# One engine instead of two for the low parts of the expert weights: all subtracted on VectorE, none on GpSimd

## Chip, cores, metric

One core of one Trainium2 chip. The metric is the device time of one execution in microseconds (us), median over repeated executions.

## What is computed

Three layers in a row. A clustered attention over `q`, `k`, `v` (2 x 8 heads, 768 positions, 64 wide) gives 1536 tokens of 512. A dense layer, 512 to 2048 and back, follows. The third layer routes each token to one of eight experts or past all of them; this is where the change lies:

```python
do_compute = x @ w_skip > 0
xc = x[do_compute]
logits = xc @ w_gate
e_idx = argmax(logits, axis=1); gate_w = softmax(logits)[e_idx]
for e in range(8):
    mask = e_idx == e
    h = maximum(xc[mask] @ w1[e], 0)          # w1[e]: 512 x 1024
    y[mask] = gate_w[mask, None] * (h @ w2[e])  # w2[e]: 1024 x 512
out = x.copy(); out[do_compute] = xc + y
```

## The kernel before

Everything is written out by hand in program order; each engine runs its own instructions strictly in that order, and semaphores hold one engine for another.

**Precision.** Matrix products in the two expert layers run in a rounded 32-bit type (`fp32r`). To keep accuracy each operand is held as two numbers: a high part, the rounded copy, and a low part, the source minus the high part. A product is then three matmuls: high x high, high x low, low x high. For weights, ScalarE (ACT) makes the high part by a copy (line 919), and VectorE (DVE) or GpSimd (POOL) the low part by a subtraction (line 921). In names of the profile `xh`, `phi` are high parts, `xl`, `plo` low parts, both in the third layer eight buffers in turn (six are reused from the first layer's tokens, two are new, `phi`/`plo`); `rawa`, `rawb` are the weights as loaded.

**The third layer.** An expert's weights are four chunks of 128 x 4 x 512 numbers, 1 MB each: two of `w1`, two of `w2`. The work is a list of 32 *stages*, one chunk each: `u` (up: tokens times half of `w1`, lines 1069 to 1081) and `d` (down: activations times half of `w2`, line 1105). The order is up of expert 0, then up of expert 1, down of expert 0, up of 2, down of 1, and so on, with the eighth expert at the end; a leftover tile of 32 tokens (`xx_...`) is computed on an expert chosen at run time ahead of the last one. In the loop over stages (line 1268 on) one turn does, in this order: the 12 matmuls of the stage on TensorE (PE); on `u` stages the transposes of the previous expert's activations (`h_trans`: PE, high part on ACT, low part `hTl` on DVE); on `d` stages the combine `y` (DVE, line 1112) with its scatter (POOL, line 1114) or the transposed tokens of an expert two later (`x_prep`, low part `xTl` on DVE); four steps of the remaining routing work (`extras`, small DVE operations such as `en` and `ohx`); and last the split of the chunk three stages ahead (`split_stage(n + 3)`).

**The split.** `split2` (line 913) cuts a chunk into two halves of 128 x 1024. A counter `n` runs over all halves. For each, ACT makes the high part and the low part goes to POOL where `n % 8` is in `pool_n`, else to DVE. Stages 0 and 1 are split during the end of the dense layer with `pool_n=range(8)`, all on POOL (lines 993, 1009); stage 2 with `pool_n=()` (line 1049); stages 3 to 31 are split in the loop with the default. After the split the chunk's buffer is refilled by a DMA on SP's queue (`refill`, line 546), for the chunk eight later; that DMA waits for the halves' subtractions. POOL's queue also holds the gathers of tokens (line 1039) and the scatters. Matmuls of a stage wait for its low parts, and the low parts of activations stand behind the splits on DVE.

The lines that set where a low part is made:

```python
            eng = nc.gpsimd if n % 8 in pool_n else nc.vector
            eng.tensor_tensor(out=lo, in0=src, in1=_f(hi), op=ALU.subtract)
```

Of the kernel before, what the change touches and what calls it, by code (L numbers as in the profile page):

```python
# [20 lines left out]
def _f(ap):  # L21
    return ap.bitcast(F32)
# [3 lines left out]
def kernel(  # L26
# [32 lines left out]
    def pool(name, side=None, **kw):  # L59
        return tc.alloc_tile_pool(name=name, side=side, bufs=1, reuse_waits="tile", **kw)  # L60
# [17 lines left out]
    def ps_m(shape, name, dt=F32):  # L78
        return psum.tile(shape, dt, tag="M", name=name, bufs=1)

# [1 line left out]
    ident = const.tile([P, P], F32, name="ident")  # L82
    make_identity(nc, ident)
    identb = const.tile([P, P], BF16, name="identb")
    nc.vector.tensor_copy(identb, ident)

# [1 line left out]
    HS = S // 2  # L88
    nat = {}
    first = {}  # L90
# [517 lines left out]
    pieces = [(c, a_) for c in range(2, 8) for a_ in range(4)]  # L608
# [16 lines left out]
    for s in range(NSTEP + 16):  # L625
        p, r = divmod(s, 12)
# [40 lines left out]
    for i in range(2):  # L667
        m1_up(i, ps_s("ups")[:, i, :])

# [1 line left out]
    att.release()  # L671
    psum.release()
    psum = pool("psum2", None, space=PSUM)
# [55 lines left out]

    NI = NBLK * NFC  # L730

# [1 line left out]
    EMPTY = 2048.0  # L733
    XP = 32
    wg = rt.tile([P, KD, 32], F32, name="wg")
# [166 lines left out]
        V.tensor_tensor(out=g, in0=g, in1=ga[:, 3, :], op=ALU.add)  # L902
        V.tensor_scalar(out=g, in0=g, scalar1=1.0 / 1024.0, scalar2=None, op0=ALU.mult)

# [1 line left out]
    xhb = xh.rearrange("p c n -> p (c n)").rearrange("p (k a f) -> p k a f", a=2, f=512)  # L906
    xlb = xl.rearrange("p c n -> p (c n)").rearrange("p (k a f) -> p k a f", a=2, f=512)
    NXB = KD * NTOK // 1024
# [1 line left out]
    pc_t = {}  # L910
    nsp = [0]

    def split2(e, r, pool_n=(1, 4, 6)):
        for j in range(2):
            n = nsp[0]
            nsp[0] += 1
            src = chunks[8 + 4 * e + r][:, 2 * j:2 * j + 2, :]
            hi, lo = his[n % len(his)], los[n % len(los)]
            nc.scalar.activation(out=hi, in_=src, func=AF.Copy)  # L919
            eng = nc.gpsimd if n % 8 in pool_n else nc.vector  # L920
            eng.tensor_tensor(out=lo, in0=src, in1=_f(hi), op=ALU.subtract)  # L921
            pc_t[e, r, 2 * j] = hi[:, 0, :], lo[:, 0, :]
            pc_t[e, r, 2 * j + 1] = hi[:, 1, :], lo[:, 1, :]
# [15 lines left out]
    def split_stage(n, hold=False, **kw):  # L939
        if n >= len(stages):  # L940
            return
        k_, e, h = stages[n]
        r = h if k_ == "u" else 2 + h
        split2(e, r, **kw)
        if not hold:
            refill(8 + 4 * e + r)
# [103 lines left out]
    m1.release()  # L1050
    wip[0].release()

# [1 line left out]
    m2 = pool("m2", "right")  # L1054
    for k_ in range(2):
        his.append(m2.tile([P, 2, 512], F32R, name=f"phi{k_}"))
# [217 lines left out]
    for n, (k_, i, h) in enumerate(stages):  # L1274
# [9 lines left out]
        else:  # L1284
            down_half(i, h)
            if h == 1:
                e = pos_of[i]
# [28 lines left out]
    with tc.For_i(0, nreg, 1):  # L1316
        nc.vector.tensor_scalar(out=itc, in0=itc, scalar1=1.0, scalar2=None, op0=ALU.add)
        for _ in pick_expert():
            pass
        e = NPOS  # L1320
        for r in range(4):
            load_chunk(8 + 4 * e + r)
        for _ in tile_list(iota1, 1):
            pass
        gather(e, xi[:, 0:1])
        x_prep(e)
        for r in range(2):
            split2(e, r)
            up_half(e, r)
        for r in range(2):  # L1330
            h_trans(e, r)
        for r in range(2):
            split2(e, 2 + r)
            down_half(e, r)
        combine(e, xgx, xi[:, 1:2])
# [27 lines left out]
```

## Time and profile before

| | |
|---|---|
| device time, median of 3 runs (us) | 721.02 (718.91 to 723.09) |
| span of the profiled execution (us) | 722.5 |
| PE busy | 662.2 us, 92% |
| DVE busy | 478.7 us, 66% |
| ACT busy | 420.0 us, 58% |
| POOL busy | 374.4 us, 52% |
| bytes read from HBM | 66.18 MB, 103 GB/s over the span |

The profile records one execution; of its time the page gives the span, from the first to the last instruction, which lies within the range of the three runs. Busy shares are means over the whole program, and its three layers use the engines differently: the attention ends near 330 us, the dense layer near 570, the third layer takes the rest. A stretch has to be read by itself. The page's chain that ended last holds only the final scatter and says nothing of the layer ahead of it. DVE is VectorE, ACT is ScalarE, POOL is GpSimd, PE is TensorE, SP is the queue that issues most DMAs.

### The profile page before, as it was taken

What the parts mean: (1) busy time and instruction counts of PE and PEld (TensorE: products, weight loads), DVE (VectorE), ACT (ScalarE), POOL (GpSimd) and SP (SyncE); (2) the same over time, 40 slices, a digit from 0 to 9 for tenths busy, and PEclk for the clock granted to TensorE, in tenths of its full rate; (3) what the DMA queues carried; (4) which work ended last, traced back from release to release, by engine and by line L of the source; (5) the groups of instructions that cost most, each with busy time, mean ns of one, the idle gap of its engine ahead of it and who ended that gap; (6) DMA issues with size and microseconds to landing.
All of it is one profiled execution on the core that took longest, in us unless ns stands there. A gap on an engine that the chain in (4) does not pass through costs nothing. (4 is left out here: it accounts for less than half of the span.)

```text
span 722.5 us, 10397 instructions
## 1 busy us (share of the span) xinstructions
PE 662.2 (92%) x3571; PEld 494.3 (68%) x3571; DVE 478.7 (66%) x861; ACT 420.0 (58%) x808; POOL 374.4 (52%) x327
## 2 busy tenths in 40 slices
PE   5899999999999996688899999999999898888895
PEld 4666666666666664566688887888887676666665
DVE  5967877687777788999823225432245459999963
ACT  5787887888887854344444444444443547446741
POOL 4454654646553346656674444454342586346843
PEclk9999999999999999899999999999999979889999
DMA  8643635437231024443002000042333388767950
GB/s 197 144 115 74 186 104 133 128 75 185 75 105 63 30 82 152 147 134 128 0 2 117 1 1 1 0 140 94 116 117 101 133 303 291 242 218 252 325 183 24
DMA packets 58773, 88.83 MB, mean 123 GB/s; under 512 B 26745, under 2 KB 30203, under 8 KB 58720
## 3 DMA queue, kind: packets, MB, share of 16 engines
q1 hardware_dynamic: 56688, 81.79, 36.8%
q0 software_dynamic: 2032, 6.37, 2.4%
q8 instruction: 29, 0.48, 0.3%
q14 instruction: 24, 0.20, 0.1%
HBM read 66.18 MB, written 8.45 MB: 103 GB/s over the span
## 5 line engine op out<-in xcount | busy, mean ns | idle before, releaser
L343 DVE TENSOR_REDUCE st<-sps 128x1 f32<-128x768 f32 x96 | 91.6, 955 | 54.2 <-PE sps L340 43.7
L389 ACT ACTIVATE pt<-tps 128x384 f32<-128x384 f32 x192 | 83.8, 491 | 32.5 <-PE tps L382 32.0
L692 DVE TENSOR_TENSOR g<-ups,lk 128x512 f32<-128x512 f32 x48 | 33.0, 688 | 97.4 <-ACT lk L691 97.3
L603 PE MATMUL ups<-xh,wloi 128*128 128x512 f32 x192 | 78.5, 409 | 15.6 <-POOL wloi L579 15.5
L354 ACT ACTIVATE pr<-sps,st 128x768 f32<-128x768 f32 x96 | 87.0, 906 | 8.5 <-DVE st L358 4.3
L579 POOL TENSOR_TENSOR wloi<-rawb,whii 128x512 fp32r<-128x512 f32 x36 | 50.3, 1399 | 76.2 <-ACT whii L577 76.2
L397 PE MATMUL avps<-pt,vnat 128*64 128x384 f32 x384 | 81.8, 510 | 0.0
L603 PE MATMUL ups<-xh,whii 128*128 128x512 f32 x192 | 77.5, 404 | 2.3 <-ACT whii L577 2.3
L367 POOL TENSOR_SCALAR pr<-pr,st 128x768 f32<-128x768 f32 x48 | 47.9, 999 | 60.1 <-DVE st L362 53.5
L382 PE MATMUL tps<-ident,pr 128*128 128x128 f32 x576 | 78.7, 273 | 0.0
L693 ACT ACTIVATE gh<-g 128x512 fp32r<-128x512 f32 x48 | 30.4, 633 | 80.7 <-DVE g L692 80.7
L603 PE MATMUL ups<-xl,whii 128*128 128x512 f32 x192 | 77.0, 401 | 0.0
L708 PE MATMUL acc<-whio,gh 128*128 128x512 f32 x184 | 73.9, 402 | 2.1 <-ACT gh L693 2.1
L708 PE MATMUL acc<-whio,gl 128*128 128x512 f32 x184 | 72.1, 392 | 0.6 <-POOL gl L695 0.6
L382 PEld LDWEIGHTS tps<-ident,pr 128*128 128x128 f32 x576 | 68.4, 140 | 5.6 <-ACT pt L389 1.2
L708 PE MATMUL acc<-wloo,gh 128*128 128x512 f32 x184 | 72.0, 391 | 0.0
L603 PEld LDWEIGHTS ups<-xh,wloi 128*128 128x128 f32 x192 | 37.6, 196 | 27.5 <-POOL wloi L579 19.8
L691 ACT ACTIVATE lk<-ups 128x512 f32<-128x512 f32 x48 | 28.4, 591 | 45.4 <-PE ups L603 45.4
L921 DVE TENSOR_TENSOR xl<-rawb,xh 128x1024 fp32r<-128x1024 f32 x26 | 52.7, 2052 | 1.3 <-ACT xh L919 1.3
L589 POOL TENSOR_TENSOR wloo<-rawb,whio 128x512 fp32r<-128x512 f32 x36 | 50.1, 1392 | 0.9 <-ACT whio L588 0.8
L603 PEld LDWEIGHTS ups<-xh,whii 128*128 128x128 f32 x192 | 37.3, 194 | 12.2 <-ACT whii L577 4.8
L603 PEld LDWEIGHTS ups<-xl,whii 128*128 128x128 f32 x192 | 37.2, 194 | 7.9
(293 smaller groups left out, 1487.9 us busy)
## 6 DMA issues: line engine op xcount, KB each, us to landing
rawb<-in_moe_w_dram SPq DMA_DIRECT2D x26, 1024.0 KB, 5.4
stg<-in_moe_w_in_dram SPq DMA_DIRECT2D x16, 512.0 KB, 4.2
stg<-in_moe_w_out_dram SPq DMA_DIRECT2D x16, 512.0 KB, 4.0
rawa<-in_moe_w_dram SPq DMA_DIRECT2D x8, 1024.0 KB, 7.4
vnat<-in_v_dram SPq DMA_DIRECT2D x8, 384.0 KB, 3.4
x_scratch<-x SPq DMA_DIRECT2D x6, 512.0 KB, 2.6
out_dram<-x SPq DMA_DIRECT2D x6, 512.0 KB, 3.6
UB<-UA SPq DMA_DIRECT2D x15, 192.0 KB, 3.0
```

Source lines behind the costliest of these rows:

```text
L343: nc.vector.tensor_reduce(out=st[:, 0:1], in_=ps[:, :, 0:HS], axis=AX.XY, op=ALU.max, negate=True)
L354: nc.scalar.activation(out=pr, in_=ps[:, :, 0:HS], func=AF.Exp, bias=st[:, 0:1], accum_out=st[:, 1:2])
L367: nc.gpsimd.tensor_scalar(out=pr, in0=pr, scalar1=st[:, 2:3], scalar2=0.0, op0=ALU.mult, op1=ALU.add)
L382: nc.tensor.transpose(ps[:, t, :], pr[:, kh, t * P:(t + 1) * P], ident)
L389: nc.scalar.activation(out=pt[:, 3 * kh:3 * kh + 3, j, :], in_=t_t[s][kh], func=AF.Copy)
L397: nc.tensor.matmul(av_t[g][64 * h:64 * h + 64, :], lhsT=vnat[p][:, h, kt, :], rhs=pt_t[p, half, h][:, kt].rearrange("p j c -> p (j c)"), s ...
L579: eng.tensor_tensor(out=lo, in0=src, in1=_f(hi), op=ALU.subtract)
L589: nc.gpsimd.tensor_tensor(out=lo, in0=src, in1=_f(hi), op=ALU.subtract)
L603: nc.tensor.matmul(ps, lhsT=w[:, cc, :], rhs=x[:, cc, cs], start=(n == 0), stop=(n == 3 * KD - 1))
L692: nc.vector.tensor_tensor(out=g, in0=ps, in1=t, op=ALU.max)
L708: nc.tensor.matmul(ps, lhsT=a[:, ts_], rhs=w, start=(fc == 0 and n == 0), stop=(fc == NFC - 1 and n == 2))
L921: eng.tensor_tensor(out=lo, in0=src, in1=_f(hi), op=ALU.subtract)
```

## The change

The default of one argument changes: in the loop over stages, and in the loop behind it that runs only when more tiles are left over, no half goes to POOL any more. The remaining edits remove comments.

```diff
-    def split2(e, r, pool_n=(1, 4, 6)):
+    def split2(e, r, pool_n=()):
         for j in range(2):
             n = nsp[0]
             nsp[0] += 1
```

What follows shows the order of instructions on two engines, each row a line of the kernel, an operation, what it writes and reads, and a count.

DVE at the turns of the first stages, where expert 1's up halves are multiplied; rows with + are of the change, with - of before (`plo_5985`, `plo_5987` are the two new low buffers):

```order
 L1067 TENSOR_TENSOR xTl<-xT,xTh 128x512
+L921 TENSOR_TENSOR plo_5985<-rawb,phi_5984 128x1024
 L921 TENSOR_TENSOR plo_5987<-rawb,phi_5986 128x1024
 L1081 TENSOR_SCALAR h<-hps 128x512
-L921 TENSOR_TENSOR xl<-rawb,xh 128x1024
+L921 TENSOR_TENSOR xl<-rawb,xh 128x1024 x2
 L1090 TENSOR_TENSOR hTl<-hT,hTh 128x512
```

Each chunk's two subtractions now stand together on DVE, ahead of the next `h` or `hTl`.

POOL from the end of the gathers to the second scatter, before:

```order
L1039 DMA xg<-x_scratch,idx_g 128x512 x6
L921 TENSOR_TENSOR plo_5985<-rawb,phi_5984 128x1024
L921 TENSOR_TENSOR xl<-rawb,xh 128x1024
L921 TENSOR_TENSOR xl<-rawa,xh 128x1024
L921 TENSOR_TENSOR plo_5985<-rawa,phi_5984 128x1024
L1114 DMA out_dram<-y,idx_s 1536x512
L921 TENSOR_TENSOR xl<-rawb,xh 128x1024 x2
L921 TENSOR_TENSOR plo_5985<-rawb,phi_5984 128x1024
L1114 DMA out_dram<-y,idx_s 1536x512
```

and POOL from the last work of the dense layer to the end, with the change:

```order
L921 TENSOR_TENSOR xl<-rawa,xh 128x1024 x4
L1039 DMA xg<-x_scratch,idx_g 128x512 x2
L546 DMA rawa<-in_moe_w_dram 128x4x512 x2
L1039 DMA xg<-x_scratch,idx_g 128x512 x6
L1114 DMA out_dram<-y,idx_s 1536x512 x4
L1230 DMA xxg<-x_scratch,xi 128x128
L1114 DMA out_dram<-y,idx_s 1536x512 x2
```

The 22 subtractions of the stage loop are gone from POOL; its four of stages 0 and 1 and its DMAs stay in their order. PE, ACT and SP keep theirs.

## Rows read from the trace of the kernel before

Times are microseconds from the start of the span unless marked ns.

**Rows 1.** Busy time by stretch: PE, PEld, DVE, ACT, POOL, clock, DMA share, GB/s; x is instructions.

```profile
core 0: us, PE busy (x) PEld busy (x) DVE busy (x) ACT busy (x) POOL busy (x), PEclk, DMA share, GB/s
580.00:600.00 20.00, 18.15 (x86) 14.70 (x85) 12.96 (x27) 10.31 (x15) 13.34 (x12) 0.85 0.93 335
600.00:620.00 20.00, 14.78 (x63) 11.45 (x62) 19.66 (x31) 10.66 (x13) 11.88 (x5) 0.83 0.69 240
620.00:640.00 20.00, 14.96 (x63) 11.77 (x62) 19.86 (x35) 9.85 (x12) 8.20 (x4) 0.84 0.64 227
```

**Rows 2.** Waits of PE from 589 to 716 us: total, times, longest.

```profile
PE yps L1105 <- DVE xl L921: 11.2, 3, 5.2
PE yps L1105 <- DVE hTl L1090: 5.5, 2, 3.3
```

**Rows 3.** Line 921 by engine: shortest/median/longest ns, first and last start.

```profile
L921 DVE TENSOR_TENSOR xl<-rawb,xh x26: 1206/1221/6486, 577.0 to 703.1; 128x1024 fp32r<-128x1024 f32 x26
...
L921 POOL TENSOR_TENSOR xl<-rawb,xh x10: 2364/2434/3449, 592.9 to 702.2; 128x1024 fp32r<-128x1024 f32 x10
```

**Rows 4.** Timeline 609.6 to 616.1 us: start, us, engine, line, idle before.

```profile
609.59 6.49 DVE L921 TENSOR_TENSOR xl<-rawb,xh 128x1024 fp32r<-128x1024 f32 x1
...
610.30 4.68 POOL L921 TENSOR_TENSOR xl<-rawb,xh 128x1024 fp32r<-128x1024 f32 x2
...
616.13 0.79 PE L1105 MATMUL yps<-xl,hTh 128*128 128x512 f32 x1 [5.22 <-DVE xl L921]
```

**Rows 5.** Stretches A and B: line 921 alone (DVE, POOL), then all engines.

```profile
589.11:647.09 57.98, 28.88 (x16) 25.89 (x10) 0.88 0.73 255
647.09:692.54 45.45, 35.08 (x16) 25.62 (x9) 0.96 0.78 274
...
589.11:647.09 57.98, 47.34 (x216) 37.41 (x215) 54.77 (x78) 33.33 (x40) 28.56 (x13) 0.88 0.73 255
647.09:692.54 45.45, 38.56 (x186) 29.22 (x188) 44.35 (x40) 29.85 (x37) 31.04 (x13) 0.96 0.78 274
```

**Rows 6.** Timeline of DVE from 636.2 to 640 us, no POOL subtract running.

```profile
636.23 0.86 DVE L1148 TENSOR_SCALAR ohx<-iotax,jt 128x128 f16<-128x128 f32 x4
637.01 2.34 DVE L921 TENSOR_TENSOR xl<-rawb,xh 128x1024 fp32r<-128x1024 f32 x2
639.28 0.68 DVE L1081 TENSOR_SCALAR h<-hps 128x512 f32<-128x512 f32 x1
639.88 0.67 DVE L1090 TENSOR_TENSOR hTl<-hT,hTh 128x512 fp32r<-128x512 f32 x1
```

**Rows 7.** Timeline of DVE: third and sixth combine.

```profile
646.43 0.74 DVE L1112 SCALAR_TENSOR_TENSOR y<-yps,gts,xg 128x512 f32<-128x512 f32 x1
...
691.87 0.75 DVE L1112 SCALAR_TENSOR_TENSOR y<-yps,gts,xg 128x512 f32<-128x512 f32 x1 [0.31 <-PE yps L1105]
```

**Rows 8.** Groups of DVE from 589 to 647 us: busy, mean ns, idle before.

```profile
L1148 DVE TENSOR_SCALAR ohx<-iotax,jt 128x128 f16<-128x128 f32 x12 | 7.5, 689 | 0.0
...
L1183 DVE TENSOR_TENSOR en<-en 128x1 f32<-128x1 f32 x7 | 3.6, 509 | 0.2
...
L1214 DVE TENSOR_SCALAR jt<-jt 128x12 f32<-128x12 f32 x1 | 2.1, 2095 | 0.0
```

**Rows 9.** Timeline of PE: first matmul of four stages.

```profile
598.03 0.48 PE L1105 MATMUL yps<-xh,hTh 128*128 128x512 f32 x1
...
604.13 0.39 PE L1076 MATMUL hps<-xh,xTh 128*128 128x512 f32 x1
...
660.70 0.39 PE L1076 MATMUL hps<-xh,xTh 128*128 128x512 f32 x1
...
667.01 0.48 PE L1105 MATMUL yps<-xh,hTh 128*128 128x512 f32 x1
```

**Rows 10.** Timeline: ScalarE's wait for a load; SP's last loads.

```profile
681.65 2.01 ACT L919 ACTIVATE xh<-rawa 128x1024 fp32r<-128x1024 f32 x2 [0.39 <-DMA rawa<-in_moe_w_dram]
...
693.76 0.93 SPq L546 DMA_DIRECT2D rawb<-in_moe_w_dram  x2
```

## Prediction

> **What bounds the kernel now.** The change touches only the second expert layer, so I went first to the table of busy time by stretch, for the last 140 us [rows 1]. Between 600 and 640 us VectorE (DVE) is busy 19.66 and 19.86 of 20 us, while TensorE (PE) has 14.78 and 14.96 and the granted clock falls to 0.83 and 0.84, a mix of its two levels (1.2 and 2.4 GHz). An engine as full as that sets the pace. The list of waits says what PE lacks there: 11.2 us in three waits for the low half `xl` of line 921, and 5.5 us in two for `hTl`, a low half of the activations, also made on DVE [rows 2].
>
> Next I asked whether DVE really does 20 us of work. The durations of line 921 say no: on DVE the shortest and the median of the largest group are 1206 and 1221 ns, but the longest is 6486 ns, for the same shape [rows 3]. The timeline around that longest one shows why. DVE starts it at 609.59; GpSimd (POOL) starts two subtracts of line 921 at 610.30 that last 4.68 us, to 614.98; DVE's one ends at 616.08, which is 1.10 us after that, about one undisturbed duration; and PE, idle 5.22 us, goes on at 616.13 [rows 4]. Nothing in the code makes the one subtract need the other. So in these rows a POOL subtract and a DVE subtract do not run beside each other: one holds the other up. POOL needs 2434 ns (median) for what DVE does in 1221 [rows 3].
>
> **What is removed.** 22 POOL subtracts vanish: 10 between 589.11 and 647.09 us (stretch A), the other 12 after it, 9 of them before 692.54 (stretch B); 25.89 + 25.62 us of POOL time go there [rows 5]. POOL keeps the four of stages 0 and 1, which run at the end of the first layer, and its indirect DMAs, which then stand behind fewer instructions and cost nothing new.
>
> **What is added.** 22 subtracts on DVE. Two back to back take 2.34 us, so one follows the next after about 1.14 us and is itself 1.21 long [rows 3, 6]. No semaphore is new to PE, but the order changes: `h`, `hTl`, `xTl` and `y`, in line on DVE, now always stand behind two subtracts, and on SP's queue the refill of a buffer waits for both of them. What that costs is DVE's time, counted next.
>
> Stretch A runs from the low half of expert 1's tokens to the end of the third combine (`y`, starts 646.43 [rows 7]). DVE is busy 54.77 of 57.98 us [rows 5]; it is the bound, so its time is the sum:
> - Line 921: 16 now take 28.88 us [rows 5]; 26 at 1.21 make 31.5: +2.6.
> - `ohx`: 12 take 7.5 us now [rows 8]; four undisturbed ones took 0.86 [rows 6], so 12 take 2.6: -4.9.
> - `en`, seven additions of one column, take 3.6 us at 509 ns each [rows 8]; another small one, `jt` at line 1214, takes 2.1 for 12 columns [rows 8]. Both stand where POOL subtracts run. At an estimated 0.15 each, from how little work there is against `ohx` at 0.215: -2.6 and -1.9.
> - Ten more instructions overlap their neighbours by 0.07: -0.7.
> - DVE's own idle time, 57.98 - 54.77 = 3.2 us, mostly waits for ScalarE that follow a stall of PE: about 0.7 stays, -2.5.
>
> That is -10.0. I take -9.5, since a few tenths must come back where DVE meets ScalarE's high half. The bounds of this term: -10.0 above, and -4.5 if each of the 26 came out at 1.4, a third of the way from the undisturbed 1.21 to the present mean of 28.88 / 16 = 1.8 (26 x 0.19 = 5 us lost). I take the undisturbed price because POOL has no other work here that lasts.
>
> Stretch B, three more experts up to the combine that starts at 691.87 [rows 7], is 45.45 us now. Three candidates for its new length:
> - DVE: per expert 8 subtracts x 1.14, four operations out of PSUM x 0.60 (`h` to `hTl` [rows 6]), one combine of 0.66 (it starts at 646.43 [rows 7], and A ends with it): 12.2; three times that and an estimated 0.8 for eight small operations at the end of the routing work: 37.3.
> - PE at its full clock: two up stages with their transposes from 660.70 to 667.01, two down stages with theirs from 598.03 to 604.13 [rows 9]: 6.31 + 6.10 = 12.4 per expert, 37.2 for three.
> - The weight loads: 274 GB/s x 45.45 us = 12.45 MB [rows 5]; at the 335 GB/s of 580 to 600 us [rows 1] that is 37.2. (The Trainium skill, DMA: Bandwidth & Descriptors, section Specifications, puts a core's limit at about 358 GB/s from HBM; by that figure the estimate would be 34.8 and the loads could not bind. No row holds that rate over such a stretch.)
>
> All three come out alike, so the gain is at most -8.0. I take -7.5: three chains so even will hold each other up a little. Its bounds are -8.0 and the -2.5 of rival 1. For A the same load sum is 255 x 57.98 = 14.8 MB, 44 us at 335 GB/s, below the 48 that DVE wants.
>
> After B come the last 30 us: the leftover tile of the expert, the last expert, the scatter and the end. There PE never waits on line 921 and DVE has gaps; three subtracts more, 3.6 us, lie in those gaps: 0. The last two weight loads leave at 693.76, right after PE's leftover-tile matmuls [rows 10], and move with PE.
>
> **Sum:** -9.5 - 7.5 + 0 = -17.0 us. The profiled execution spans 722.5 us, 1.5 above the median of the runs, 721.0; its rows carry over. 721.0 - 17.0 = **704.0**.
>
> **What is late next.** After the change no engine of this stretch is clearly slowest: DVE 12.2 per expert, PE 12.4, loads 12.4. ScalarE, some 30 us busy of 45 [rows 5], is no candidate.
>
> **Rivals.**
> 1. *The loads become the bound.* For: the load rate must rise from 274 to 334 GB/s (12.45 MB in 37.3 us) in B. The only long stretch that shows 335 had 93% of the transfer engines' time in use [rows 1], and no row shows that rate held for 100 us. Against: in the whole stretch ScalarE waits for a load once, 0.39 us [rows 10], and loads are asked for eight chunks, two experts, ahead. At 305 GB/s B takes 40.8 and A 48.5, giving 707; at 290, 42.9 and 51.0, giving -2.5 - 7.0, so 711.5. Middle **709**.
> 2. *Slower: DVE is simply full, and 22 more subtracts on it lengthen the layer.* If the long durations came from something that stays (the loads into SBUF, ScalarE's reads), the added ones would cost what the present ones do: 10 x 28.88/16 = 18.1 us in A and about 9 x 35.08/16 = 19.7 in B [rows 5], less 4.3 us of idle time: +33.5, so **754.5**. It decides from the point where 50 subtracts exceed the present 64.0 us and that idle time: a mean of (64.0 + 4.3) / 50 = 1.37 us. Against: undisturbed ones are 1.21, and the longest ends when POOL lets go [rows 3, 4, 6]. The Trainium skill takes both sides. Its page Perfetto Trace Analysis, section Optimizing Scalar/DVE Operations, says that with VectorE saturated, offloading work even to GpSimd may make sense, and that the port the two share may undo it; its first half speaks against this change and gives this rival. Its page SBUF — State Buffer, section Who interferes with whom, says that a VectorE instruction with two SBUF inputs and a GpSimd one that reads SBUF contend, and the loser blocks fully; by that the long durations go with POOL's subtracts and the forecast's -17 stands. This trace agrees with the second [rows 4].
> 3. *No change:* PE's waits for `xl` turn into waits for `hTl`, which now always stands behind two subtracts of DVE's own. It is in DVE's sum already, so it would need PE and DVE to wait for each other in turn: **720**.
>
> **Chances.** Forecast 0.72 (698 to 708), rival 1 0.18 (706 to 712), a part of the blocking staying 0.03 (712 to 717), rival 3 0.03, rival 2 0.04. A change of 0.5%, 3.6 us, is about what a measurement of this kernel can tell from none. Faster by more: 0.72 + 0.18 + 0.03 = 0.93; within it 0.03; slower 0.04.
>
> **Range.** Best case: PE never stalls. From 604.13 to 660.70 [rows 9] it does the twelve stages of three experts, which at its full clock are 37.2 us instead of 56.6: -19.4. The eight stages from there to 691.87 would be 24.8 instead of 31.2: -6.4. That floor, 695, leaves DVE's sum out, which ends at -18; the stretch ahead of 604 us and a shorter end could add a few us to it, so I go to 698. Worst of the likely cases: rival 1 at 290 GB/s, 711.5. So **698 to 712**.
>
> **What would show it.** In the profile after: every line 921 on DVE at 1.2 us, no duration over 1.5 after 590 us, and no POOL subtract there; `ohx` and `en` at 0.2 and 0.15; PE's waits for `xl` near 0; the granted clock near 1.0 from 600 to 640; three combines in some 38 us where [rows 7] have 45.4; the rate of the loads above 300 GB/s. The forecast is wrong if DVE's subtracts stay bimodal without POOL, if ScalarE's waits for loads grow to several us, or if PE's waits come back under another name.

## Result and the profile after

| | before | after |
|---|---|---|
| device time, median of 4 runs each (us) | 722.06 (718.91 to 723.38) | 702.82 (702.16 to 703.44) |
| span of the profiled execution (us) | 722.5 | 700.9 |
| DVE busy (us) | 478.7 | 465.7 |
| POOL busy (us) | 374.4 | 322.9 |

The ratio of after to before is 0.9746, 95% interval 0.9709 to 0.9782: 19.2 us less. DVE has 22 instructions more and is busy 13 us less.

Line 921 in the profile after, one row for each pair of buffers: shortest, median and longest duration in ns, then the first and last start.

```profile
L921 DVE TENSOR_TENSOR xl<-rawb,xh x36: 1212/1217/1227, 576.0 to 682.3; 128x1024 fp32r<-128x1024 f32 x36
...
L921 DVE TENSOR_TENSOR plo<-rawb,phi x8: 1215/1218/1227, 589.0 to 686.4; 128x1024 fp32r<-128x1024 f32 x8
L921 DVE TENSOR_TENSOR xl<-rawa,xh x8: 1210/1216/1225, 599.5 to 668.4; 128x1024 fp32r<-128x1024 f32 x8
L921 DVE TENSOR_TENSOR plo<-rawa,phi x8: 1209/1216/1226, 603.0 to 671.3; 128x1024 fp32r<-128x1024 f32 x8
L921 POOL TENSOR_TENSOR xl<-rawa,xh x4: 2372/2412/2419, 562.3 to 569.4; 128x1024 fp32r<-128x1024 f32 x4
```

Against [rows 3]: the spread is gone. All 60 subtracts on DVE last 1209 to 1227 ns; the long ones, up to 6486, went with POOL's. POOL keeps its four ahead of the layer.

The table by stretch (the columns of [rows 1]), and under it the two stretches of the prediction, A and B, at their new places: from the `xTl` at 588.04 to the end of the third combine at 635.83, and to that of the sixth at 673.06.

```profile
600.00:620.00 20.00, 19.26 (x91) 15.09 (x90) 19.62 (x43) 15.09 (x20) 1.03 (x1) 1.00 0.90 299
620.00:640.00 20.00, 17.93 (x88) 14.02 (x87) 19.93 (x40) 11.86 (x15) 1.99 (x2) 0.91 0.88 308
640.00:660.00 20.00, 20.00 (x97) 16.43 (x97) 20.00 (x22) 16.76 (x20) 5.42 (x2) 1.00 0.99 338
...
588.04:635.83 47.79, 44.98 (x214) 35.50 (x213) 46.98 (x88) 33.34 (x40) 2.75 (x3) 0.96 0.90 305
635.83:673.06 37.23, 37.23 (x206) 29.89 (x205) 37.16 (x49) 30.12 (x38) 9.27 (x4) 1.00 0.97 339
```

DVE is as full as before, but of work: A takes 47.79 us instead of 57.98 and B 37.23 instead of 45.45 [rows 5]. In B, PE is busy 37.23 of 37.23 us and DVE 37.16. Loads ran at 339 GB/s there with 97% of the transfer engines' time in use, and the granted clock is 1.00.

The waits of PE in the layer (total us, times, longest), against 11.2 and 5.5 us in [rows 2]:

```profile
PE yps L1105 <- DVE hTl L1090: 1.2, 1, 1.2
PE yps L1105 <- DVE xl L921: 0.8, 1, 0.8
PE yps L1105 <- DVE nxi L1200: 0.5, 1, 0.5
PE yps L1105 <- DVE exi L1134: 0.2, 1, 0.2
```

And on DVE's timeline the small operations that [rows 8] had at 7.5 and 3.6 us in all: eight `ohx`, and four of the seven `en`.

```profile
602.36 0.73 DVE L1183 TENSOR_TENSOR en<-en 128x1 f32<-128x1 f32 x4
...
621.25 1.68 DVE L1148 TENSOR_SCALAR ohx<-iotax,jt 128x128 f16<-128x128 f32 x8
```

### The profile page after: what moved, and what is told of

Read it like the earlier page. It is cut to its first block, busy times and chain, and to the rows that moved or that the text cites. A ratio compares the mean times of both kernels' runs of the same rounds, so it can differ in the third digit from the quotient of the medians.

```text
span 700.9 us, 10375 instructions
## 1 busy us (share of the span) xinstructions
PE 655.1 (93%) x3571; PEld 491.6 (70%) x3571; DVE 465.7 (66%) x883; ACT 419.9 (60%) x808; POOL 322.9 (46%) x305
## 5 line engine op out<-in xcount | busy, mean ns | idle before, releaser
L603 PE MATMUL ups<-xh,wloi 128*128 128x512 f32 x192 | 77.7, 405 | 15.9 <-POOL wloi L579 15.9
L691 ACT ACTIVATE lk<-ups 128x512 f32<-128x512 f32 x48 | 28.4, 592 | 49.0 <-PE ups L603 49.0
L603 PEld LDWEIGHTS ups<-xh,wloi 128*128 128x128 f32 x192 | 37.2, 194 | 26.5 <-POOL wloi L579 18.9
L1114 POOL DMA_INDIRECT out_dram<-y,idx_s x8 | 13.5, 1693 | 79.1 <-DVE y L1112 36.0
L603 PEld LDWEIGHTS ups<-xh,whii 128*128 128x128 f32 x192 | 37.2, 194 | 11.5 <-ACT whii L577 4.1
L921 DVE TENSOR_TENSOR xl<-rawb,xh 128x1024 fp32r<-128x1024 f32 x36 | 42.3, 1218 | 0.3 <-ACT xh L919 0.3
```

The source lines that it names most:

```text
L603: nc.tensor.matmul(ps, lhsT=w[:, cc, :], rhs=x[:, cc, cs], start=(n == 0), stop=(n == 3 * KD - 1))
```

## Experiments

All times are medians of four runs, beside seven of the kernel before; the ratio is to the kernel before, and differences are taken to the changed kernel's 702.82 us. The changed kernel itself was not run beside them. The kernel before had a median of 722.06 us beside it, 722.43 beside the first four experiments and 723.07 beside the last four, so a difference of about 1 us says little.

### POOL's subtractions given back as idle ones

```diff
             eng.tensor_tensor(out=lo, in0=src, in1=_f(hi), op=ALU.subtract)
+            if 6 <= n < 64 and n % 8 in (1, 4, 6):
+                nc.gpsimd.tensor_tensor(out=scr[0], in0=_f(hi), in1=_f(hi), op=ALU.subtract)
```

> The changed kernel, plus 22 idle subtractions on POOL where the removed ones stood; each reads a high part twice and writes a scratch tile that nothing reads. Theory (a POOL subtract holds up DVE): every one costs DVE up to its own 2.4 us, as in the profile before. Stretch A, 47.8 us in the profile after, grows by 10 x 2.4 = 24, stretch B, 37.2, by 9 x 2.4 = 22: 735 to 750 us, and DVE's line 921 shows durations of 2.2 to 6.5 us again. Rival (the gain came from PE no longer waiting for low parts that POOL finishes late, 2.4 against 1.2 us): nobody waits for the scratch tile, so 703, within 1 us, and all of line 921 at 1.2 us.

Measured: 729.16 us (727.89 to 730.35), ratio 1.0098 (1.0062 to 1.0134): 26.3 us more than the changed kernel, and 1% above the kernel before. Line 921 is line 922 here, the idle subtract 924. The durations, and the timeline at the same point of the work as [rows 4]:

```profile
L922 DVE TENSOR_TENSOR xl<-rawb,xh x36: 1206/1216/3740, 576.3 to 708.9; 128x1024 fp32r<-128x1024 f32 x36
...
609.93 6.57 DVE L922 TENSOR_TENSOR xl<-rawb,xh 128x1024 fp32r<-128x1024 f32 x2
...
610.64 1.93 POOL L924 TENSOR_TENSOR scr<-xh 128x1024 fp32r<-128x1024 f32 x1
...
612.75 2.67 POOL L924 TENSOR_TENSOR scr<-xh 128x1024 fp32r<-128x1024 f32 x1 [0.18 <-ACT xh L920]
...
613.72 0.79 PE L1110 MATMUL yps<-xl,hTh 128*128 128x512 f32 x1 [2.46 <-DVE xl L922]
```

Two DVE subtracts that should take 2.35 us take 6.57 while POOL does two that nobody needs, and PE waits 2.46 us for the first of them. This rules the rival out: the time is not lost by PE's waiting for low parts which POOL finishes late, since here no one waits for POOL's subtracts. The size was off. The first `xTl`, the third and the sixth combine of this run:

```profile
586.50 0.69 DVE L1072 TENSOR_TENSOR xTl<-xT,xTh 128x512 fp32r<-128x512 f32 x1 [0.20 <-ACT xTh L1071]
...
649.54 0.74 DVE L1117 SCALAR_TENSOR_TENSOR y<-yps,gts,xg 128x512 f32<-128x512 f32 x1
...
699.12 0.74 DVE L1117 SCALAR_TENSOR_TENSOR y<-yps,gts,xg 128x512 f32<-128x512 f32 x1
```

A is 63.0 us from start to start (586.50 to 649.54) against 47.1 in the changed kernel (588.04 to 635.17), B 49.6 against 37.2: 15.9 us for 10 POOL subtracts and 12.4 for 9, so 1.4 to 1.6 us each and not the 2.4 of the expectation. What an idle subtract takes from DVE is less than its length; part of it runs while DVE does the operations whose source is PSUM, and the row at 612.75 shows POOL's second subtract itself stretched, to 2.67 us.

### Work on POOL that reads almost nothing

```diff
+            if 6 <= n < 64 and n % 8 in (1, 4, 6):
+                nc.gpsimd.tensor_scalar(out=scr[1], in0=_f(hi)[:, 0, 0:1], scalar1=1.0, scalar2=1.0, op0=ALU.mult, op1=ALU.mult)
+                for _ in range(2):
+                    nc.gpsimd.memset(scr[0], 0.0)
```

> As the first, but where it subtracts, POOL copies one column of the high part (so that it starts at the same point of the work) and fills a scratch tile of 128 x 1024 twice, which reads nothing. If what DVE loses is lost to any POOL work of that length, the time is near that of the first decoy, for as long as the fills last. If it is lost only to POOL instructions that read the state buffer beside a DVE instruction with two inputs there, as the Trainium skill, SBUF - State Buffer, section Who interferes with whom, has it, the line 921 durations stay at 1.2 us and the time at 703 to 705.

Measured: 704.72 us (703.60 to 706.34), ratio 0.9761 (0.9725 to 0.9797): 1.9 us more than the changed kernel. The groups of POOL in the layer (busy us, mean ns, idle before), and line 921 (922 here):

```profile
L926 POOL MEMSET scr<- 128x1024 f32 x44 | 42.0, 954 | 1.3
...
L922 DVE TENSOR_TENSOR xl<-rawb,xh x36: 1206/1218/1231, 576.8 to 683.2; 128x1024 fp32r<-128x1024 f32 x36
```

POOL is busy for 42.0 us with the fills alone, in the same places, and no DVE subtract is longer than 1231 ns. So a subtract on DVE loses nothing to fills; it loses to POOL's subtracts, which read. The Trainium skill, SBUF — State Buffer, section Who interferes with whom, states just that for a VectorE instruction with two inputs in SBUF, and the subtracts of these two runs agree. A long POOL instruction with one input was not tried.

Fills and one-column copies are not free for every DVE operation. Most of the remaining 1.9 us lies at one place, the eight `ohx`: 3.02 us here, 1.68 in the changed kernel, while POOL ran a copy and two fills:

```profile
620.93 3.02 DVE L1156 TENSOR_SCALAR ohx<-iotax,jt 128x128 f16<-128x128 f32 x8
...
622.35 0.57 POOL L924 TENSOR_SCALAR scr<-xh 128x1 f32<-128x1 f32 x1
622.87 1.98 POOL L926 MEMSET scr<- 128x1024 f32 x2
```

That is 1.3 us, as much as A is longer than in the changed kernel (48.5 us from start to start against 47.1); B is 37.2 in both. Which of the two kinds held `ohx` up is not shown.

### The change undone stretch by stretch

```diff
-            eng = nc.gpsimd if n % 8 in pool_n else nc.vector
+            eng = nc.gpsimd if n % 8 in pool_n or (6 <= n < 32 and n % 8 in (1, 4, 6)) else nc.vector
```

with `6 <= n < 32` for A, `32 <= n < 56` for B and `56 <= n < 64` for the end of the layer.

> The changed kernel with the 10 subtractions of stretch A (halves 6 to 31) split as before, 3 in 8 on POOL. Theory: A returns to 58 us from 47.8 in the profiles, so +10 us: 711 to 714. B and the end stay at 37.2 and 27.8. If the gain were a matter of both stretches together (loads that run ahead, say), less than 5 us comes back.

> The changed kernel with the 9 subtractions of stretch B (halves 32 to 55) split as before. Theory: B returns to 45.4 us from 37.2: +8, 709 to 712, A stays at 47.8. With the kernel that has A split as before, the two should add up to all but 1 or 2 us of the whole difference of 19 us.

> The changed kernel with the last 3 subtractions (halves 56 to 63) split as before. The prediction put their move at nothing, since DVE has gaps there: 702 to 704. If the 1.6 us that the end of the layer lost between the two profiles (22.96 to 21.35 us from the sixth combine's end to the last scatter's issue) came from them, 704.5 or more.

Measured: A undone 713.99 us (712.64 to 716.92), ratio 0.9893 (0.9854 to 0.9933), +11.2. B undone 709.43 (708.51 to 712.81), 0.9833 (0.9794 to 0.9873), +6.6. The end undone 703.54 (702.40 to 703.98), 0.9722 (0.9699 to 0.9745), +0.7, within the spread of the runs. Together 18.5 of the 19.2 us. Measured from the kernel before that ran beside each, they are +10.8, +6.2 and -0.3, together 16.7. The third and sixth combine with A undone, and with B undone:

```profile
646.76 0.74 DVE L1112 SCALAR_TENSOR_TENSOR y<-yps,gts,xg 128x512 f32<-128x512 f32 x1
...
683.97 0.75 DVE L1112 SCALAR_TENSOR_TENSOR y<-yps,gts,xg 128x512 f32<-128x512 f32 x1
```

```profile
634.46 0.74 DVE L1112 SCALAR_TENSOR_TENSOR y<-yps,gts,xg 128x512 f32<-128x512 f32 x1
...
678.87 0.74 DVE L1112 SCALAR_TENSOR_TENSOR y<-yps,gts,xg 128x512 f32<-128x512 f32 x1
```

From start to start B is 37.2 us where A alone was undone, and 44.4 where B was. Each stretch keeps its own price to within about 1 us, so it is in the main a matter of the stretch's own blocking and not of a lead that one hands to the next.

### Less on DVE: one half of the ReLU on ACT

```diff
-            nc.vector.tensor_scalar(out=h_t[e][:, 1, :], in0=ps, scalar1=0.0, scalar2=None, op0=ALU.max)
+            nc.scalar.activation(out=h_t[e][:, 1, :], in_=ps, func=AF.Relu)
```

> The changed kernel with the second half of each expert's ReLU (line 1081) on ACT instead of DVE: 0.60 us less on DVE per expert, as much more on ACT. If DVE is still the bound in stretch A, as its 19.62 and 19.93 us of 20 in the profile after say, A gets 4 x 0.6 = 2.4 us shorter; in stretch B PE is as full as DVE (20.00 of 20 from 640 to 660 us), so 0 to 0.5 there: 700 to 701. If PE or the loads now set the pace throughout, 702.8 as before, or worse if ACT becomes late.

Measured: 701.33 us (700.15 to 702.27), ratio 0.9701 (0.9677 to 0.9724): 1.5 us less. In its profile A is 46.1 us from start to start, 1.0 less, and B 36.3, also 1.0 less:

```profile
586.46 0.69 DVE L1067 TENSOR_TENSOR xTl<-xT,xTh 128x512 fp32r<-128x512 f32 x1 [0.41 <-ACT xTh L1066]
...
632.55 0.75 DVE L1112 SCALAR_TENSOR_TENSOR y<-yps,gts,xg 128x512 f32<-128x512 f32 x1
...
668.81 0.74 DVE L1112 SCALAR_TENSOR_TENSOR y<-yps,gts,xg 128x512 f32<-128x512 f32 x1
```

That is under half of the 2.4 expected in A. DVE was nearly all of A's bound but not alone; PE's work of 45.0 us in A (the fourth row of the table by stretch) stands close behind. In B the expectation of at most 0.5 was too low, and with it the reading that PE is B's floor: PE was busy for all of B's 37.23 us in the changed kernel, and yet B got shorter when DVE had less to do. The table by stretch for B here:

```profile
632.55:668.81 36.26, 36.11 (x195) 29.00 (x197) 35.65 (x45) 30.70 (x40) 9.28 (x4) 1.00 1.00 357
```

The total says less. The profiled span is 2.5 us shorter (698.4 against 700.9); 1.6 of that lies ahead of A, in code that the edit does not touch, and 1.1 of the 2.0 from A and B is lost again from the sixth combine to the end (29.6 us against 28.5). About 0.9 is left for the edit. By the medians it is 1.5, or 2.5 from the kernel before that ran beside it.

### The same move at the start of the dense layer

Up to 355 us each step decodes weights on DVE in four operations of two instructions (lines 515 to 527), while POOL makes the low parts `wloi`, `wloo` and `gl`. All three move to DVE, behind the decodes of their step:

```diff
+    def low(eng, out, a, b):
+        if 0 <= loop_i[0] <= 10:
+            late.append(lambda: nc.vector.tensor_tensor(out=out, in0=a, in1=_f(b), op=ALU.subtract))
+        else:
+            eng.tensor_tensor(out=out, in0=a, in1=_f(b), op=ALU.subtract)
...
         conv_next(2 * i + PRE)
+        for f in late:
+            f()
+        late.clear()
```

> The same move in another place: at the start of the dense layer (300 to 360 us) DVE decodes weights in four operations of two each per step while POOL does three subtractions of 128 x 512 (wloi, wloo, gl) of 1.7 us. In the profile after, the decodes of line 523 take 3.45 us a pair beside them and 1.28 alone, and DVE is busy all the time at 8.15 us per step. With the three on DVE, behind the decodes of their step (steps 0 to 10), a step needs 0.60 + 0.67 + 3 x 1.21 + 3 x 0.63 = 6.8 us: about 1.35 x 6 = 8 us less, 693 to 698. If PE's waits for wloi there have another cause, or the low parts now come too late behind the decodes, 702 to 708.

Measured: **688.30 us** (687.89 to 689.43), ratio 0.9521 (0.9498 to 0.9544): 14.5 us less than the changed kernel. One step of DVE in the changed kernel (from `g` to `g`, lines 692), then one here (lines 700):

```profile
338.70 0.68 DVE L692 TENSOR_TENSOR g<-ups,lk 128x512 f32<-128x512 f32 x1
339.30 0.75 DVE L515 TENSOR_SCALAR cvt<-stg 128x512 uint32<-128x512 uint32 x2
339.97 2.38 DVE L519 SCALAR_TENSOR_TENSOR cvt<-stg,cvt 128x512 uint32<-128x512 uint32 x2
342.28 3.47 DVE L523 SCALAR_TENSOR_TENSOR cvt<-stg,cvt 128x512 uint32<-128x512 uint32 x2
345.68 1.28 DVE L527 SCALAR_TENSOR_TENSOR rawb<-cvu,cvt 128x512 f32<-128x512 f32 x2
346.88 0.68 DVE L692 TENSOR_TENSOR g<-ups,lk 128x512 f32<-128x512 f32 x1
```

```profile
307.98 0.69 DVE L700 TENSOR_TENSOR g<-ups,lk 128x512 f32<-128x512 f32 x1
308.58 0.76 DVE L515 TENSOR_SCALAR cvt<-stg 128x512 uint32<-128x512 uint32 x2
309.25 1.29 DVE L519 SCALAR_TENSOR_TENSOR cvt<-stg,cvt 128x512 uint32<-128x512 uint32 x2
310.45 1.29 DVE L523 SCALAR_TENSOR_TENSOR cvt<-stg,cvt 128x512 uint32<-128x512 uint32 x2
311.65 1.29 DVE L527 SCALAR_TENSOR_TENSOR rawb<-cvu,cvt 128x512 f32<-128x512 f32 x2
312.86 0.69 DVE L575 TENSOR_TENSOR gl<-g,gh 128x512 fp32r<-128x512 f32 x1
313.46 0.69 DVE L575 TENSOR_TENSOR wloi<-rawb,whii 128x512 fp32r<-128x512 f32 x1
314.06 0.69 DVE L575 TENSOR_TENSOR wloo<-rawb,whio 128x512 fp32r<-128x512 f32 x1
314.66 0.69 DVE L700 TENSOR_TENSOR g<-ups,lk 128x512 f32<-128x512 f32 x1
```

The step falls from 8.18 to 6.68 us with three instructions more on DVE, as worked out (8.15 to 6.8). The total was underestimated because I counted six such steps; the code has ten (two pieces of weights each from step 1 to 10). From the `g` of step 1 to that of step 11 they take 81.6 us in the changed kernel (273.42 to 355.02) and 66.9 here (274.54 to 341.39): 14.7 less. From the kernel before that ran beside it the gain is 15.5.

### Both

> The two before it in one kernel. They lie in different layers, so they should add up: some 10 us under the changed kernel, 691 to 696.

Measured: 688.00 us (687.60 to 688.79), ratio 0.9510 (0.9489 to 0.9531). The ReLU's 1.5 us do not show on top: 0.3 less than without it, inside the spread. In the layer itself it is there: from the second `xTl` to the sixth combine this profile takes 82.9 us, and 84.4 without the ReLU's move. It is lost on either side. From the first `xTl` to the second it takes 5.03 us here and 4.03 without (the ten profiles lie between 3.97 and 5.54, and the edit does not touch this code), and from the sixth combine to the end 29.3 against 28.4. What sets these two stays open.

## Why the prediction was right

The forecast was 704.0 us, 17.0 less than before; measured are 702.82 and 19.2 less.

- **What bounded the layer.** DVE, full with blocked time. Shown by the idle subtracts, which bring the long durations back without changing what anyone needs, and by the fills, beside which every subtract stays short.
- **Stretch A, forecast -9.5 of a sum of -10.0.** By the profiles -10.2 (57.98 to 47.79), by undoing it +11.2 (10.8 from the kernel before beside it). The terms: 26 subtracts 30.6 us by DVE's time in line 921 against 31.5; 12 `ohx` 1.68 + 0.86 = 2.5 against 2.6; four `en` 0.73, so about 0.18 each against the estimate of 0.15.
- **Stretch B, forecast -7.5 with three candidates between 37.2 and 37.3 us.** 37.23 us, -8.2 by the profiles, 6.6 by undoing it. My allowance for three even chains holding each other up was not needed: PE did not stop once. But the three were not equal floors. With 0.6 us less on DVE per expert, B took 36.26 us, below the 37.2 that I had put down for PE and for the loads alike; DVE's 37.3 was the candidate that held.
- **The end of the layer, forecast 0.** Its three subtracts: 0.7 us by undoing them, not to be told from nothing. But from the sixth combine to the last scatter's issue the profile after is shorter, 21.35 us against 22.96 (from 673.06 to 694.41, and from 692.54 to 715.50). I put that down to where the cut lies and not to work saved: in the changed kernel PE runs ahead of DVE's combine, and has begun the leftover tile, at 670.68, 1.7 us before that combine starts:

```profile
670.68 1.93 PE L1244 MATMUL xxh<-rawb,xxT 128*32 128x256 f32 x32
672.40 0.74 DVE L1112 SCALAR_TENSOR_TENSOR y<-yps,gts,xg 128x512 f32<-128x512 f32 x1
```

  Before, that combine waited 0.31 us for PE [rows 7], so the two were level. So some of the gain of A and B seems to lie behind my boundary; that is the term of 0 which was 1.6 off.
- **The base.** I set the profiled span 722.5 beside the median of 721.0 and took 1.5 for the difference. The profiled execution after took 702.66 us with a span of 700.9, 1.8 more than its span. In the runs of the kernel before that stand beside the experiments it was 1.8 to 2.0, so the profiled execution before took some 724.4 by estimate, 2.3 over the median of 722.06 and 3.4 over the 721.0 that I started from. That the forecast is 1.2 us from the measured time, while the gain is 2.2 off, is luck in part: the base was 1.0 too low. The 21.6 us between the two spans hold 1.1 that came before the layer (`xTl` starts at 588.04 and 589.11) and lie in code that did not change.
- **Rival 1, the loads.** Not the bound: ACT never waited for a load, though the median from issue to landing rose from 5.6 to 6.6 us. B ran at 339 GB/s with 97% of the transfer engines' time in use, and that was not the most they give. With less on DVE, B ran at 357, and in the profile after 20 us of it were faster still:

```profile
645.00:665.00 20.00, 20.00 (x100) 16.50 (x99) 20.00 (x23) 15.79 (x21) 8.29 (x3) 1.00 1.03 372
```

  The Trainium skill, DMA: Bandwidth & Descriptors, section Specifications, gives about 358 GB/s as a core's limit from HBM. All transfers of this core together ran above that here, at 372; the weight loads alone, 7.09 MB of them, at 354.
- **Rival 2, DVE simply full.** Fell: it needed a mean of 1.37 us per subtract and got 1.22. (Its price was a little low: of the 16 subtracts that the row of B counts on DVE, the last begins at the boundary; with 15 the price is 755.8.) Of the two pages of the Trainium skill that the prediction set against each other, SBUF — State Buffer, section Who interferes with whom, was borne out, as far as the subtracts go.
- **Rival 3, waits under another name.** PE's waits for `hTl` fell too, from 5.5 to 1.2 us.
- **The clock.** The sign held in part: 1.00 from 600 to 620 us, but 0.91 from 620 to 640. From 622 to 626 PE was busy for 1.94 of 4 us, waiting for `xl` and `hTl` behind the eight `ohx`, and from 626 to 628 the granted clock was 0.50.

## What to carry to other kernels

A second engine is no help for work on which it holds up the first: look for one instruction shape with a short median and a long tail, and see what runs beside the long ones. Here 22 subtractions moved onto the engine that was already 98 to 99% busy from 600 to 640 us, and its busy time went down. The same tail in another place of the same kernel was worth another 14.5 us.

## What was not expected of the hardware

It goes the other way too. The eight scatters on POOL in the profile after have a shortest and a median issue of 982 and 1017 ns, but a longest of 2866 (1732 in the kernel before); on the timeline the longest meets two subtracts on DVE:

```profile
L1114 POOL DMA_INDIRECT out_dram<-y,idx_s x8: 982/1017/2866, 606.3 to 694.4; - x8
...
660.92 2.35 DVE L921 TENSOR_TENSOR xl<-rawb,xh 128x1024 fp32r<-128x1024 f32 x2
...
661.29 2.87 POOL L1114 DMA_INDIRECT out_dram<-y,idx_s  x1 [6.41 <-DVE y L1112]
```

It ends at 664.16, 0.89 us after DVE's pair ended (660.92 + 2.35 = 663.27), so it seems to have stood still until then. Three of the eight scatters took 2.85 to 2.87 us, and each of them began about 0.36 us after a pair of subtracts. Two that began 0.3 and 0.5 us ahead of a pair (606.33 and 636.19, the pairs at 606.65 and 636.66) took 1.03 and 0.98. Nobody waited for a scatter here, and one that someone waits for would be another matter; that was not tried. The one-column copies on POOL show it too: the shortest took 190 ns and the longest 1987.

Nor did I expect a DVE subtract that the trace shows as started to be overtaken: in [rows 4] DVE's began 0.71 us before POOL's first and ended after POOL's second. In the trace before this happened also to those that start at 647.91 and 679.31, and each of the three began while POOL was issuing a scatter, with a subtract right behind it. Others kept their 1.23 us although POOL's subtract began before they ended: the one at 603.06, with no indirect DMA on POOL, and the one at 665.73, while POOL was issuing a gather. What decides it stays open; the start that the trace shows does not.
